# An attention and gated-MLP kernel: g factored as columns, root chains and v's split on GpSimd, the last block stored by halves

## The chip, the cores and the metric

The kernel runs on one core of one Trainium2 chip. The metric is the device time of the program in microseconds. TensorE, VectorE, ScalarE and GpSimd work side by side, each in its own order; SP issues most transfers.

## The reference

Eight batches with twelve heads of 448 positions and 64 columns go through attention with normalised queries and keys; the heads are joined to 768 columns and go through a gated channel MLP with a shift by one position. All data are float32 in the reference except what the inputs bring as 64-bit numbers: the three weight matrices.

```python
def rmsnorm(x, g):
    rms = np.sqrt(np.mean(x * x, axis=-1, keepdims=True) + 1e-06)
    return x / rms * g
q_n, k_n = (rmsnorm(q, g_q), rmsnorm(k, g_k))
scores = scale * np.matmul(q_n, k_n.transpose(0, 1, 3, 2))
attn = softmax(scores)
x = np.matmul(attn, v)                  # then joined to [8, 448, 768]
x_prev = shift(x)                       # one position later, zero first
xk = mu_k * x + (1.0 - mu_k) * x_prev
xr = mu_r * x + (1.0 - mu_r) * x_prev
k = np.maximum(xk @ w_k, 0.0)           # w_k 768 x 1024
v = k * k @ w_v                         # w_v 1024 x 768
r = 1.0 / (1.0 + np.exp(-(xr @ w_r)))   # w_r 768 x 768
return r * v
```

## The kernel before, in words

**Units and pairs.** Four heads of a batch are a unit (24 units, `u`), two heads a pair (48). A unit's k and q come as [128, 896] tiles: two heads in each half of the partitions, seven times 64 positions. `load` issues these transfers in order on SP (half of unit 0 on ScalarE's queue), `vload` those of v.

**Roots.** `stats` squares k and q (ScalarE), folds 64 columns to 32 (GpSimd), sums them (VectorE, `sst`), adds epsilon and takes the inverse root by eight small VectorE steps (`rsqrt`, line 464), whose first and fifth results lie in PSUM (`root`, a corner of the bank `last`). Unit 0 takes one chain for k and one for q; every later unit one for both, 28 columns wide. From unit 3 on (`U32`) the epsilon carries a factor from g.

**Preparing k and q.** `preps` multiplies by the roots. The first six units (`PE_T`) are then turned by TensorE (`turn`), later ones by transposing transfers. [...] The factor g_q g_k / 8 goes on k: in `turn` as one number per partition, `gc` (column 0 for the first three units, column 1, scaled by a power of g's size, for the next three), from unit 6 on as the row `G`. `setup` makes both: one product spreads g_q and g_k over the partitions, VectorE multiplies them, picks the diagonal and reduces it to `gc`, then computes the scale `gm` by a chain of one-column steps.

**Attention.** `scores` issues the products of a group (seven groups per unit) into PSUM banks `sc`; `expo` takes the row maximum (VectorE) and the exponential with its sum (ScalarE); `probs` and `split` scale and split the probabilities and turn them by transfers, or `probs_pe` by TensorE (the first 21 groups, with reciprocals in `rc`); `attends` multiplies by v in bank `last`; `settle` evacuates to `x`, for the first three units with a product that spreads the reciprocals.

**v.** `vprep` finds a power of two for v (square sum on ScalarE or maximum on VectorE, a product with an identity, a reduction, two or three steps on the bits) and from unit 3 on splits v: high part on ScalarE (line 876), low part on VectorE (line 877).

**Weights.** `wload`, `weights` and `wsplit` load 20 column slices (8 of w_k, 6 of w_r, 6 of w_v), turn their 64-bit numbers to float32, find a power of two per slice (a Gram product, its diagonal by a product with `ident`, a float32 product with ones over 128 columns, a reduction, two steps on the bits) and split them to float16, by GpSimd and ScalarE or by ScalarE and VectorE, whichever clock is behind (`LEAN_W`).

**MLP.** `mixk` and `mixr` mix x with its shift (`mix`); `moe` waits until all six pairs of a batch are mixed and all of w_k is split, multiplies by w_k, squares (`square`), and then goes over blocks of 128 rows: for each half `h` of the 768 columns the product with w_r, `gate` (tanh on ScalarE in three pieces), the product with w_v, `store`.

**What sets the order.** All of this is written as Python generators. A planner (`Plan`, line 240) keeps an estimated clock for each engine and picks at each step the operation that can start first, shifted by priorities: the constants at the head of the file, and `FIRST` and `SECOND`, which hold before batch 0's and batch 1's MLP. The instructions are then issued in that order on each engine, so an instruction that waits holds those behind it on its engine. `plan.over(a, b, d)` and `plan.lean(d)` choose an engine by these clocks. The end of a block is

```python
yield V.scalar_tensor_tensor(out=th, in0=th, scalar=1.0, in1=zv[:, 0:NH], op0=ALU.add, op1=ALU.mult)
yield G_.tensor_tensor(out=th, in0=th, in1=spread(rsu[...], P), op=ALU.mult)
if len(OC) == 2:
    for e, (r, tt) in enumerate(dst):
        yield SP.dma_start(out=r[tt], in_=o[e * HD:(e + 1) * HD, :])
```

(shortened: both halves of a block leave together, as two transfers of 64 rows).

Of the kernel before, what the change touches and what calls it, by code (L numbers as in the profile page):

```python
# [69 lines left out]
XK_AT = 2  # L70
SC_AHEAD = 0
PRIO_Q = -119
PRIO_V = 295
MARGIN = 560
MARGIN_A = 196
MARGIN_V = 569
# [8 lines left out]
BOOST_K = 564
BOOST_R = 792
BOOST_A = -32
BOOST_W = 398
# [3 lines left out]
BOOST_V = -31  # L92
SLACK_V = 2
PRIO_W = 195
W_START = 6979.55
W_G0 = -9
W_G1 = 0
PRIO_L = 233
# [14 lines left out]
LEAD_V = 0  # L113
# [80 lines left out]
def price(op):  # L194
# [5 lines left out]
    if e == "DVE":  # L200
        two = "in1" in kw
        c = n / 0.96 + (128 if two and n >= 64 and (not ps or any(SIZE[x.dtype] == 2 for x in aa)) else 64)
        return c, c + 80
# [9 lines left out]
    if "in1" in kw:  # L213
        c = n * (2.15 if kw["out"].dtype == F16 else 2.0) + 40
    else:
        c = n * 0.83 + 223
# [246 lines left out]

def rsqrt(V, y, a, t, w=None):
# [8 lines left out]
    yield V.scalar_tensor_tensor(out=y, in0=t, scalar=9.0 / 16, in1=w[1], op0=ALU.add, op1=ALU.mult)  # L473


def attn_moe_kernel(tc, q, k, v, g_q, g_k, mu_k, mu_r, w_k, w_v, w_r, out):
# [26 lines left out]
    gd = gk  # L503
# [93 lines left out]
    def setup():  # L597
# [25 lines left out]
        yield V.tensor_scalar(out=gm[:, 0:1], in0=gm[:, 0:1], scalar1=TINY, scalar2=None, op0=ALU.max)  # L623
        yield from rsqrt(V, gm[:, 1:2], gm[:, 0:1], gm[:, 5:6])
        yield V.tensor_scalar(out=G, in0=G, scalar1=gm[:, 1:2], scalar2=None, op0=ALU.mult)
        yield V.tensor_tensor(out=gc[:, 1:2], in0=gc[:, 0:1], in1=gm[:, 1:2], op=ALU.mult)
        yield V.tensor_tensor(out=gm[:, 2:3], in0=gm[:, 1:2], in1=gm[:, 1:2], op=ALU.mult)
        yield V.tensor_scalar(out=gm[:, 6:7], in0=gm[:, 1:2], scalar1=HD ** -0.5, scalar2=None, op0=ALU.mult)
        st["gm"] = True
        yield V.tensor_scalar(out=eps[:, 2 * NT:], in0=eps[:, 2 * NT:], scalar1=gm[:, 2:3], scalar2=None, op0=ALU.mult)  # L630

    def mu_stats():
# [48 lines left out]
    def stats():  # L681
        for u in range(NQ):
# [3 lines left out]
            for n, t in enumerate(LD[u]):  # L686
# [18 lines left out]
                if u == 0 or n:  # L705
# [7 lines left out]
                    if u:  # L713
                        SS[u, 0] = y
# [667 lines left out]
```

## Time and profile before

| | |
|---|---|
| median of three runs | 980.72 us (980.3 to 982.4) |
| profiled execution | 979.14 us |
| its span, first to last instruction | 977.4 us |
| TensorE matmul busy | 915.2 us (94%) |
| VectorE busy | 772.8 us (79%) |
| ScalarE busy | 756.3 us (77%) |
| GpSimd busy | 589.9 us (60%) |
| mean granted TensorE clock | 0.982 |

Busy time of TensorE is the time in which at least one matmul is under way; a matmul's own duration overlaps with that of the next. Shares over the whole span mix stages: a head in which heads are prepared and weights are split, a long middle with MLP and attention side by side, and an end with MLP products alone. [...] "Idle before" is the time an engine stood before an instruction, with what released it.

### The profile page before, as it was taken

To read this page: it belongs to the slowest core of one execution; us is meant where nothing else is said; L and a number is where in the kernel's file an instruction comes from. 1 tells how busy PE (TensorE), PEld (TensorE's weight loads), DVE (VectorE), ACT (ScalarE), POOL (GpSimd) and SP (SyncE) were. 2 spreads that over 40 slices of the span, in tenths; PEclk is the share of its full clock that TensorE was granted. 3 is DMA by queue.
4 is the path that set the end of the run, shared out by engine and by line. 5 is a ranking of instruction groups with operands and counts; after the bars stand their busy time and mean duration, and the time that the engine had idled before them with its cause. 6 is when DMAs were issued, how large, how long until landed. Compare 5 with 4: busy or idle time off the path is not lost. (4 is left out here: it accounts for less than half of the span.)

```text
span 977.4 us, 18849 instructions
## 1 busy us (share of the span) xinstructions
PE 915.2 (94%) x6171; PEld 489.2 (50%) x6171; DVE 772.8 (79%) x2132; ACT 756.3 (77%) x1818; POOL 589.9 (60%) x593
## 2 busy tenths in 40 slices
PE   3898969899999999999999999999999999999997
PEld 2554534445545554455445554455445554555564
DVE  6899899988999999888877899897989888814100
ACT  3788799989988888898987889898899888812111
POOL 2575678746767666677675558756776456425411
PEclk9799979999999999999999999999999999999999
DMA  7654389579969999899598998999799897610011
GB/s 194 165 159 134 122 211 197 125 132 200 190 132 193 208 192 188 144 182 209 108 194 167 177 175 156 171 199 173 144 178 200 162 186 145 115 24 25 1 34 32
DMA packets 399238, 147.72 MB, mean 151 GB/s; under 512 B 349476, under 2 KB 395556, under 8 KB 399140
## 3 DMA queue, kind: packets, MB, share of 16 engines
q1 hardware_dynamic: 398852, 146.06, 75.4%
q8 instruction: 48, 0.79, 0.3%
q10 hardware_dynamic: 288, 0.46, 0.2%
q14 instruction: 50, 0.41, 0.2%
HBM read 51.52 MB, written 11.01 MB: 64 GB/s over the span
## 5 line engine op out<-in xcount | busy, mean ns | idle before, releaser
L314 PE MATMUL mm<-wvh,kk 128*128 128x384 f16 x896 | 231.8, 326 | 0.0
L314 ACT ACTIVATE sc<-sc,sums 128x448 f32<-128x448 f32 x294 | 178.7, 617 | 41.5 <-DVE sums L314 36.9
L314 PE MATMUL mm<-xk,wkh 128*128 128x448 f16 x768 | 208.9, 354 | 0.8 <-DVE kf L314 0.8
L314 DVE SCALAR_TENSOR_TENSOR nat<-sc,sums,nat 128x384 f16<-128x384 f32 (+1 forms) x448 | 185.3, 462 | 24.0 <-ACT nat L314 22.7
L314 DVE TENSOR_REDUCE sums<-sc 128x1 f32<-128x448 f32 x336 | 190.2, 612 | 5.2 <-PE sc L314 4.8
L314 PEld LDWEIGHTS <-kk 128*128 128x128 f16 (+1 forms) x1362 | 130.0, 98 | 96.1 <-issue 13.8
L314 PE MATMUL mm<-wrh,xr 128*128 128x384 f16 x672 | 176.1, 328 | 0.0
L314 ACT ACTIVATE nat<-sc,sums 128x448 f16<-128x448 f32 (+1 forms) x276 | 165.5, 657 | 4.9 <-DVE sums L314 3.2
L314 PE MATMUL mm<-wvl,kk 128*128 128x384 f16 x448 | 146.0, 326 | 0.0
L314 PE MATMUL sc<-stk 64*128 64x448 f16 (+3 forms) x1104 | 128.2, 381 | 13.3 <-DVE nat L314 3.7
L314 PE MATMUL mm<-xk,wkl 128*128 128x448 f16 x384 | 135.6, 353 | 0.0
L314 PEld LDWEIGHTS <-xr 128*128 128x128 f16 x1008 | 97.4, 98 | 69.8 <-issue 7.8
L314 PE MATMUL mm<-wrl,xr 128*128 128x384 f16 x336 | 110.1, 328 | 0.0
L314 PEld LDWEIGHTS <-wkh 128*128 128x128 f16 x768 | 72.3, 98 | 75.4 <-issue 13.6
L314 PE MATMUL last<-pT,vhl 128*64 128x448 f16 x936 | 97.1, 355 | 4.9 <-DMA pT<-nat 3.5
L314 POOL TENSOR_TENSOR o<-o,bsc 128x384 f32<-128x384 f32 x48 | 40.8, 850 | 96.4 <-DVE o L314 68.7
L314 DVE SCALAR_TENSOR_TENSOR o<-o,mm 128x384 f32<-128x384 f32 x56 | 30.6, 546 | 80.8 <-PE mm L314 73.5
L314 ACT ACTIVATE o<-mm,bsc 128x128 f32<-128x128 f32 x144 | 43.3, 386 | 60.8 <-PE mm L314 36.6
L314 POOL TENSOR_TENSOR qk<-qk,ss 128x896 f32<-128x896 f32 x36 | 61.3, 1702 | 31.5 <-DVE ss L314 25.3
L314 PEld LDWEIGHTS <-vhl 128*64 128x64 f16 x936 | 51.8, 110 | 47.6 <-issue 12.0
L314 PEld LDWEIGHTS <-stk 64*128 64x128 f16 x1008 | 35.4, 98 | 69.8 <-issue 28.0
L314 POOL TENSOR_TENSOR nat<-nat 128x448 f32<-128x448 f32 x43 | 50.8, 1182 | 31.9 <-ACT nat L314 31.7
(199 smaller groups left out, 1611.0 us busy)
## 6 DMA issues: line engine op xcount, KB each, us to landing
out_dram<-o SPq DMA_DIRECT2D x56, 192.0 KB, 3.0
qk<-in_k_dram SPq DMA_DIRECT2D x46, 224.0 KB, 3.8
qk<-in_q_dram SPq DMA_DIRECT2D x36, 192.0 KB, 3.8
raw<-in_moe_w_v_dram SPq DMA_DIRECT2D x12, 512.0 KB, 4.4
raw<-in_moe_w_r_dram SPq DMA_DIRECT2D x12, 384.0 KB, 3.7
vf<-in_v_dram SPq DMA_DIRECT2D x18, 256.0 KB, 4.0
vf<-in_v_dram SPq DMA_DIRECT2D x18, 192.0 KB, 3.8
kk<-in_moe_w_k_dram SPq DMA_DIRECT2D x8, 384.0 KB, 4.0
```

The source lines that it names most:

```text
L314: r = op.fn(op.kw["out"], op.kw["value"]) if op.fn.__name__ == "memset" else op.fn(**op.kw)
```

## The change

- **g as columns.** Four one-column products put g_q and g_k on the partitions; two ScalarE steps multiply them to `gc`, which is ready before the rows. The row `G`, the scale `gm` and its root chain go to GpSimd (`rsqrt_pool`, eleven steps on tiles in SBUF).
- **Roots.** Unit 0 takes one chain for k and q together. From unit 1 on the chain goes to GpSimd when its estimated clock is behind VectorE's (`LEAN_R`), the addition of epsilon always.
- **v.** The power of two comes from one step on the exponent byte (`halfroot`), read from PSUM where v is kept whole. From unit 3 on the split goes to GpSimd (scale, subtract) with a ScalarE copy between, when GpSimd's clock is behind (`LEAN_L`).
- **Weights.** `halfroot` takes the place of two steps; for w_r and w_v the slice's scale comes from the trace of the Gram product, in one accumulating VectorE step and a one-column product.
- **Small steps moved.** mu's steps go to GpSimd or fall away, some scales and the reciprocals' offsets in `probs_pe` go to ScalarE, one inverse to GpSimd.
- **Last block.** GpSimd adds one to the gate and applies the outer scale before the w_v product is done; VectorE multiplies; each half leaves by its own two transfers.
- **Order.** Two costs of the planner are new or changed, v's loads start one unit later (`LEAD_V`), and most priorities and leanings have other values.

```diff
-LEAN_X = 0
+LEAN_X = -11
 LEAN_K = 0
+LEAN_R = 1
+LEAN_L = -7
 LEAN_W = 0
-LEAN_Q = 3000
-LEAN_M = -3000
-LEAN_V = -3000
-LEAN_H = -3000
-LEAN_N = -3736
+LEAN_Q = 2021
+LEAN_M = -1449
+LEAN_V = -2198
+LEAN_H = -2668
+LEAN_N = -5364
...
-LEAD_V = 0
+LEAD_V = 1
...
+def halfroot(V, o, a):
+    top = a.bitcast(mybir.dt.uint8).rearrange("p (n b) -> p n b", b=4)[:, :, 3]
+    return V.tensor_scalar(out=o.bitcast(I32), in0=top, scalar1=-float(1 << 23), scalar2=float(204 << 23), op0=ALU.mult, op1=ALU.add)
...
+def rsqrt_pool(G, y, a, t, u):
+    yield G.tensor_scalar(out=y.bitcast(I32), in0=a.bitcast(I32), scalar1=-0.5, scalar2=float(0x5F3759DF), op0=ALU.mult, op1=ALU.add)
+    yield G.tensor_tensor(out=t, in0=a, in1=y, op=ALU.mult)
...
+        yield [T.matmul(form=("f", 240), out=pt[h * HD:(h + 1) * HD, 2 * HD + n:2 * HD + n + 1], lhsT=g1[:, n, :], rhs=ones[0:1, :], start=True, stop=True) for n in range(2) for h in range(2)]
         yield T.matmul(form=("f", 300), out=pt[:, 0:2 * HD], lhsT=one_row, rhs=g1.rearrange("p a d -> p (a d)"), start=True, stop=True)
-        yield A.copy(out=gq, in_=pt[:, 0:HD])
+        yield A.activation(out=gc[:, 1:2], in_=pt[:, 2 * HD:2 * HD + 1], func=AF.Copy, scale=HD ** -0.5)
+        yield A.activation(out=gc[:, 0:1], in_=pt[:, 2 * HD + 1:2 * HD + 2], func=AF.Copy, scale=gc[:, 1:2])
+        st["gc"] = True
+        yield A.activation(out=gq, in_=pt[:, 0:HD], func=AF.Copy, scale=HD ** -0.5)
         yield A.copy(out=gk, in_=pt[:, HD:2 * HD])
         banks["mm"].put(pt)
-        yield V.scalar_tensor_tensor(out=G, in0=gq, scalar=1.0 / float(HD) ** 0.5, in1=gk, op0=ALU.mult, op1=ALU.mult)
-        for h in range(2):
-            hs = slice(h * HD, (h + 1) * HD)
-            yield V.tensor_tensor(out=gd[hs, :], in0=G[hs, :], in1=ident[hs, hs], op=ALU.mult)
-        yield V.tensor_reduce(out=gc[:, 0:1], in_=gd, axis=AX.X, op=ALU.add)
-        st["gc"] = True
+        yield G_.tensor_tensor(out=G, in0=gq, in1=gk, op=ALU.mult)
...
+        yield from rsqrt_pool(G_, gm[:, 1:2], gm[:, 0:1], gm[:, 5:6], gm[:, 4:5])
+        yield G_.tensor_scalar(out=G, in0=G, scalar1=gm[:, 1:2], scalar2=0.0, op0=ALU.mult, op1=ALU.add)
...
-                if u == 0 or n:
-                    c = slice(2 * NT * n if u == 0 else 0, 2 * NT * (n + 1))
-                    if u < U32:
-                        yield V.tensor_scalar(out=ss[:, c], in0=ss[:, c], scalar1=1e-6, scalar2=None, op0=ALU.add)
+                if n:
+                    c = slice(0, NSS)
+                    E_ = G_ if u and plan.over("POOL", "DVE", LEAN_R) else V
+                    if not u:
+                        yield V.tensor_scalar(out=ss, in0=ss, scalar1=1e-6, scalar2=None, op0=ALU.add)
+                    elif u < U32:
+                        yield G_.tensor_scalar(out=ss[:, c], in0=ss[:, c], scalar1=1.0, scalar2=1e-6, op0=ALU.mult, op1=ALU.add)
                     else:
-                        yield V.tensor_tensor(out=ss, in0=ss, in1=eps, op=ALU.add)
-                    yield from rsqrt(V, y[:, c], ss[:, c], tm[:, c], (root[:, 0, c], root[:, 1, c]))
-                    SS[u, n] = y
-                    if u:
-                        SS[u, 0] = y
+                        yield G_.tensor_tensor(out=ss, in0=ss, in1=eps, op=ALU.add)
+                    if E_ is G_:
+                        yield from rsqrt_pool(G_, y[:, c], ss[:, c], tm[:, c], su[:, c])
+                    else:
+                        yield from rsqrt(V, y[:, c], ss[:, c], tm[:, c], (root[:, 0, c], root[:, 1, c]))
+                    SS[u, 0] = SS[u, 1] = y
...
+        m = vs[:, 2:3] if half else pt[:, 2 * P:2 * P + 2]
+        yield V.tensor_reduce(out=m, in_=pt[:, 0:n * P].rearrange("p (a c) -> p a c", c=P), axis=AX.X, op=ALU.max)
+        if half:
+            banks["ot"].put(pt)
...
+            yield halfroot(V, sv, m)
...
-                yield A.activation(out=hl[:, 0], in_=ve, func=AF.Copy, scale=sv)
-                yield V.scalar_tensor_tensor(out=hl[:, 1], in0=ve, scalar=sv, in1=hl[:, 0], op0=ALU.mult, op1=ALU.subtract)
+                if plan.over("POOL", "DVE", LEAN_L):
+                    yield G_.tensor_scalar(out=ve, in0=ve, scalar1=sv, scalar2=0.0, op0=ALU.mult, op1=ALU.add)
+                    yield A.copy(out=hl[:, 0], in_=ve)
+                    yield G_.tensor_tensor(out=hl[:, 1], in0=ve, in1=hl[:, 0], op=ALU.subtract)
+                else:
+                    yield A.activation(out=hl[:, 0], in_=ve, func=AF.Copy, scale=sv)
+                    yield V.scalar_tensor_tensor(out=hl[:, 1], in0=ve, scalar=sv, in1=hl[:, 0], op0=ALU.mult, op1=ALU.subtract)
...
-            yield V.tensor_scalar(out=r, in0=sums[:, 4:7:2] if u >= U32 else r, scalar1=1e-9, scalar2=2.0 ** -15, op0=ALU.add, op1=ALU.mult)
+            yield A.activation(out=r, in_=sums[:, 4:7:2] if u >= U32 else r, func=AF.Copy, scale=2.0 ** -15, bias=1e-9 * 2.0 ** -15)
...
+        if ci < NF:
+            yield V.tensor_tensor(out=dg, in0=pg[:, 0:P], in1=ident, op=ALU.mult)
+            yield T.matmul(form=("f", 400), out=pg[:, P:2 * P], lhsT=ones.broadcast_to([P, P]), rhs=dg, start=True, stop=True)
+            R["dg"].put(dg)
+            yield V.tensor_reduce(out=sc, in_=pg[:, P:2 * P], axis=AX.X, op=ALU.max)
+            banks[WB(ci)].put(pg)
+            yield halfroot(V, sc, sc)
+        else:
+            tr = small.tile([P, 1], F32, name="trace", bufs=2)
+            yield V.tensor_tensor_reduce(out=dg, in0=pg[:, 0:P], in1=ident, scale=1.0, scalar=0.0, op0=ALU.mult, op1=ALU.add, accum_out=tr)
+            R["dg"].put(dg)
+            yield T.matmul(form=("f", 250), out=pg[:, P:P + 1], lhsT=ones.broadcast_to([P, P]), rhs=tr, start=True, stop=True)
+            yield halfroot(V, sc, pg[:, P:P + 1])
+            banks[WB(ci)].put(pg)
...
-            yield V.tensor_scalar(out=RSC, in0=WIN[:, 0:NF], scalar1=wsc[:, 0:1], scalar2=RELU_SCALE, op0=ALU.mult, op1=ALU.mult)
+            yield V.tensor_scalar(out=wsc[:, 0:1], in0=wsc[:, 0:1], scalar1=RELU_SCALE, scalar2=None, op0=ALU.mult)
+            yield A.activation(out=RSC, in_=WIN[:, 0:NF], func=AF.Copy, scale=wsc[:, 0:1])
...
+                    last = b == B - 1 and blk == NT - 1
+                    plan.spawn(gate(h, zr, th, rsu, TH, last), PRIO_M)
...
+        if last:
+            yield G_.tensor_scalar(out=th, in0=th, scalar1=1.0, scalar2=1.0, op0=ALU.mult, op1=ALU.add)
+            yield outer(h, th, rsu)
         TH[0] = True
 
-    def store(h, zv, th, rsu, o, OC, dst, TH):
+    def outer(h, th, rsu):
+        t3 = th.rearrange("p (c n) -> p c n", n=P)
+        return G_.tensor_tensor(out=t3, in0=t3, in1=spread(rsu[:, ND + 3 * h:ND + 3 * h + 3], P), op=ALU.mult)
...
+        if last:
+            yield V.tensor_tensor(out=th, in0=th, in1=zv[:, 0:NH], op=ALU.mult)
+            banks["mm"].put(zv)
+            for e, (r, tt) in enumerate(dst):
+                yield SP.dma_start(out=r[tt][:, h * NH:(h + 1) * NH], in_=th[e * HD:(e + 1) * HD, :])
+            return
```

## Rows read from the trace of the kernel before

**Rows 1.** Windows: stretch, length, each engine's busy time (instructions), clock, DMA share, GB/s.

```profile
20.00:200.00 180.00, 152.01 (x1002) 83.97 (x1000) 163.40 (x436) 151.94 (x340) 121.49 (x121) 0.91 0.62 158
200.00:850.00 650.00, 636.51 (x4424) 330.87 (x4419) 572.88 (x1614) 572.54 (x1398) 421.62 (x408) 1.00 0.93 172
...
122.40:145.50 23.10, 14.24 (x99) 7.72 (x98) 20.67 (x59) 20.89 (x42) 17.50 (x17) 0.74 0.82 210
```

**Rows 2.** Timeline, 119 to 146 us: start, duration, engine, operation, tiles; [idle before <- releaser].

```profile
119.23 3.23 PE L314 MATMUL last<-pT,vf 128*64 128x448 f32 x16
...
141.22 0.68 DVE L314 TENSOR_SCALAR sc<-x,bsc 128x448 f32<-128x448 f32 x1
...
145.46 0.93 PE L314 MATMUL mm<-xk,wkh 128*128 128x448 f16 x2
```

**Rows 3.** Timeline of the first 20 us.

```profile
7.77 0.76 PE L314 MATMUL mm<-grow,ones 1*128 1x128 f32 x2 [7.77 <-DMA grow<-in_g_k_dram]
8.26 1.12 POOL L314 TENSOR_TENSOR nat<-nat 128x448 f32<-128x448 f32 x1 [0.67 <-ACT nat L314]
8.28 1.14 DVE L314 TENSOR_SCALAR sst<-sst 128x14 f32<-128x14 f32 x1
...
10.90 0.17 DVE L314 SCALAR_TENSOR_TENSOR ss<-stm,last 128x14 f32<-128x14 f32 x1
10.98 0.61 DVE L314 TENSOR_REDUCE sst<-nat 128x14 f32<-128x448 f32 x1
11.51 1.08 DVE L314 TENSOR_TENSOR nat<-xk,ss 128x896 f32<-128x896 f32 x1
...
12.74 1.73 PE L314 MATMUL sc<-ident,nat 128*128 128x128 f32 x7 [4.21 <-DVE sst L314]
...
15.69 0.69 ACT L314 ACTIVATE stk<-sc,gc 128x512 f32<-128x512 f32 x1 [6.79 <-DVE gc L314]
...
19.27 2.45 PE L314 MATMUL sc<-stk 64*128 64x448 f32 x8
```

**Rows 4.** Groups of VectorE instructions by shape, 0 to 200 us: busy us, mean ns | idle.

```profile
L314 DVE TENSOR_SCALAR WSC<-WSC 128x1 int32<-128x1 int32 x40 | 5.8, 144 | 0.2
...
L314 DVE SCALAR_TENSOR_TENSOR vhl<-vf,bstat,vhl 128x512 f16<-128x512 f32 x4 | 3.4, 838 | 0.5 <-ACT vhl L314 0.5
L314 DVE TENSOR_TENSOR dg<-mm,ident 128x128 f32<-128x128 f32 x12 | 3.3, 279 | 0.1
...
L314 DVE TENSOR_TENSOR sst<-sst,eps 128x28 f32<-128x28 f32 x4 | 2.6, 658 | 0.1
L314 DVE TENSOR_TENSOR stm<-sst,last 128x28 f32<-128x28 f32 x10 | 1.8, 180 | 0.2
...
L314 DVE TENSOR_SCALAR rc<-rc 128x8 f32<-128x8 f32 x3 | 1.4, 456 | 0.0
```

**Rows 5.** Groups of GpSimd and ScalarE instructions by shape, whole span.

```profile
L314 POOL TENSOR_TENSOR nat<-qk,nat 128x512 f16<-128x512 f32 x10 | 11.6, 1158 | 4.7 <-ACT nat L314 4.7
...
L314 POOL TENSOR_SCALAR raw<-raw 128x512 int32<-128x512 uint8 x12 | 8.3, 691 | 1.8 <-DMA raw<-in_moe_w_v_dram 1.0
...
L314 POOL COPY x<-x 128x63 f32<-128x63 f32 x24 | 5.7, 237 | 33.5 <-DVE x L314 25.6 <-ACT x L314 5.2 <-DVE sums L314 2.6
L314 POOL TENSOR_TENSOR nat<-qk,nat 128x128 f16<-128x128 f32 x13 | 5.6, 427 | 0.0
...
L314 ACT ACTIVATE bsc<-ismu,bsc 128x2 f32<-128x2 f32 x8 | 2.6, 321 | 1.1 <-DVE bsc L314 1.1
```

**Rows 6.** Timeline of the end, from 967 us.

```profile
967.66 0.89 ACT L314 ACTIVATE o<-mm,bsc 128x128 f32<-128x128 f32 x3 [5.89 <-PE mm L314]
...
971.63 0.55 DVE L314 SCALAR_TENSOR_TENSOR o<-o,mm 128x384 f32<-128x384 f32 x1 [6.19 <-PE mm L314]
972.27 0.83 POOL L314 TENSOR_TENSOR o<-o,bsc 128x384 f32<-128x384 f32 x1 [5.91 <-DVE o L314]
973.12 1.11 SPq L314 DMA_DIRECT2D out_dram<-o  x2
```

More of the change, by code (lines that the diff above doesn't have):

```diff
@@ L69 @@
 MU_AT = 1
-XK_AT = 2
+XK_AT = 3
 SC_AHEAD = 0
-PRIO_Q = -119
-PRIO_V = 295
+PRIO_Q = -127
+PRIO_V = 299
 MARGIN = 560
-MARGIN_A = 196
-MARGIN_V = 569
+MARGIN_A = 293
+MARGIN_V = 612
 PS = 0.1
@@ L80 @@
 PRIO_K = -112
-PRIO_R = 342
-PRIO_O = 57
+PRIO_R = 324
+PRIO_O = 220
 O_BUFS = 2
 PRIO_M = 490
[L85 to L88, printed above, removed]
+BOOST_K = 486
+BOOST_R = 262
+BOOST_A = -66
+BOOST_W = 222
 BOOST_Q = 898
@@ L91 @@
 SLACK_Q = 3
[L92 to L95, printed above, removed]
+BOOST_V = -66
+SLACK_V = 1
+PRIO_W = 228
+W_START = 6604.274
 W_G0 = -9
 W_G1 = 0
-PRIO_L = 233
+PRIO_L = 106
 Q_DVE = 1
@@ L201, in price @@
         two = "in1" in kw
-        c = n / 0.96 + (128 if two and n >= 64 and (not ps or any(SIZE[x.dtype] == 2 for x in aa)) else 64)
+        if kw.get("accum_out") is not None:
+            return n / 0.96 + 190, n / 0.96 + 270
+        ap = any(isinstance(kw.get(k), bass.AP) for k in ("scalar", "scalar1")) and n > 2 and SIZE[kw["out"].dtype] == 4
+        c = n / 0.96 + 60 * ap + (128 if two and n >= 64 and (not ps or any(SIZE[x.dtype] == 2 for x in aa)) else 64)
         return c, c + 80
@@ L213, in price @@
     if "in1" in kw:
-        c = n * (2.15 if kw["out"].dtype == F16 else 2.0) + 40
+        c = n * (2.15 if kw["out"].dtype == F16 else 2.0) + (40 if n > 300 else 150)
     else:
@@ L502, in attn_moe_kernel @@
     gc = const.tile([P, 2], F32, name="gc")
-    gd = gk
     NW = NF + 2 * ND
@@ L629, in setup @@
+        yield G_.tensor_tensor(out=gm[:, 2:3], in0=gm[:, 1:2], in1=gm[:, 1:2], op=ALU.mult)
+        yield G_.tensor_scalar(out=gm[:, 6:7], in0=gm[:, 1:2], scalar1=HD ** -0.5, scalar2=0.0, op0=ALU.mult, op1=ALU.add)
         st["gm"] = True
-        yield V.tensor_scalar(out=eps[:, 2 * NT:], in0=eps[:, 2 * NT:], scalar1=gm[:, 2:3], scalar2=None, op0=ALU.mult)
+        yield G_.tensor_scalar(out=eps[:, 2 * NT:], in0=eps[:, 2 * NT:], scalar1=gm[:, 2:3], scalar2=0.0, op0=ALU.mult, op1=ALU.add)
     def mu_stats():
@@ L692, in stats @@
                 yield A.activation(out=xs, in_=tv, func=AF.Square, scale=gm[:, 6:7] if n and u >= U32 else HD ** -0.5)
-                yield G_.tensor_tensor(out=xs[:, :, 0:HD // 2], in0=xs[:, :, 0:HD // 2], in1=xs[:, :, HD // 2:], op=ALU.add)
-                m = HD // 2
+                m = HD
+                if True:
+                    m //= 2
+                    yield G_.tensor_tensor(out=xs[:, :, 0:m], in0=xs[:, :, 0:m], in1=xs[:, :, m:2 * m], op=ALU.add)
                 while m > 1 and (u, n) in TREE and m > TREE_TO:
@@ L1189, in weights, with inverse @@
             plan.spawn(wsplit(nm, kt, c, ci, f), wprio)
-    def inverse(o, i):
-        return V.tensor_scalar(out=o.bitcast(I32), in0=i.bitcast(I32), scalar1=-1.0, scalar2=float(0x7F000000), op0=ALU.mult, op1=ALU.add)
+    def inverse(o, i, E=V):
+        return E.tensor_scalar(out=o.bitcast(I32), in0=i.bitcast(I32), scalar1=-1.0, scalar2=float(0x7F000000), op0=ALU.mult, op1=ALU.add)
     def wsplit(nm, kt, c, ci, f):
@@ L1201, in wsplit @@
         sc = WSC[:, ci:ci + 1]
-        sci = sc.bitcast(I32)
         dg = yield from R["dg"].get()
-        yield V.tensor_tensor(out=dg, in0=pg[:, 0:P], in1=ident, op=ALU.mult)
-        yield T.matmul(form=("f", 400), out=pg[:, P:2 * P], lhsT=ones.broadcast_to([P, P]), rhs=dg, start=True, stop=True)
-        R["dg"].put(dg)
-        yield V.tensor_reduce(out=sc, in_=pg[:, P:2 * P], axis=AX.X, op=ALU.max)
-        banks[WB(ci)].put(pg)
-        yield V.tensor_scalar(out=sci, in0=sci, scalar1=24, scalar2=23, op0=ALU.logical_shift_right, op1=ALU.logical_shift_left)
-        yield V.tensor_scalar(out=sci, in0=sci, scalar1=-1.0, scalar2=float(204 << 23), op0=ALU.mult, op1=ALU.add)
+        if ci < NF:
[5 more added lines that the diff above has]
+            yield halfroot(V, sc, sc)
+        else:
+            tr = small.tile([P, 1], F32, name="trace", bufs=2)
[4 more added lines that the diff above has]
+            banks[WB(ci)].put(pg)
         if plan.over("POOL", "DVE", LEAN_W):
@@ L1331, in square, with gate @@
         KF[f] = True
-    def gate(h, zr, th, rsu, TH):
+    def gate(h, zr, th, rsu, TH, last):
         for c in range(3):
```

54 lines of the change are left out of this document (28 added, 26 removed).

## The prediction

> **What bounds the kernel now.** I read the windows of the trace first, then the timeline where TensorE stands. From 200 us on TensorE has work nearly all the time: between 200 and 850 us it is busy 636.5 of 650 us at a granted clock of 1.00 [rows 1]. The change leaves its large products as they are, so this part can give back at most 13.5 us. Time is left in three places: the start, the head up to about 200 us, and the tail behind the last product.
>
> In the head, 20 to 200 us, TensorE is idle 180 - 152.0 = 28.0 us, and its mean clock is 0.91 [rows 1]. [...] The fullest engine there is VectorE, 163.4 of 180 us (0.908), then ScalarE with 151.9 and GpSimd with 121.5. The worst piece is 122.4 to 145.5 us: TensorE 14.2 of 23.1 us at clock 0.74, VectorE and ScalarE 20.7 and 20.9 [rows 1]. There the MLP's first product waits for batch 0's last head pair: that pair's value product starts at 119.23 and lasts 3.23, its mix comes to VectorE only at 141.22, and the MLP starts at 145.46 [rows 2]. The steps between are a few us of work; the rest is queueing on VectorE and ScalarE behind weight splits and other heads. So I take the head as bound by VectorE's load.
>
> **The start.** Today k's evacuation waits 6.79 us for `gc`, which comes through VectorE at about 15.6, and the first scores start at 19.27 [rows 3]. With the change `gc` is two one-column ScalarE steps behind the g product. That starts at 7.77 [rows 3]; allowing 0.8 for it and 2 x 0.32 for the steps (the 128x2 row of [rows 5]), `gc` is there by 9.3. The four added one-column products stand in the 4.21 us that TensorE idles before 12.74 [rows 3] and cost nothing; without that cover they cost under 1 us. The price is that k now waits for q: one chain for both. GpSimd's fold of q ends at 8.26 + 1.12 = 9.38, the reduction (0.61) at about 10.0. Eight chain steps took from 8.28 + 1.14 = 9.42 to 11.07 today, so with an addition of 0.2 they end at 11.9. The two multiplications of 1.08 end at 13.0 and 14.1, q's seven transposes (1.73) at 15.9, the last evacuation (0.69) at 16.6 [rows 3]. First scores at 16.6 instead of 19.27: -2.7 us, with 0 and -3.3 as ends. Loading v one unit later moves unit 1's k and q ahead of two pairs of v transfers in SP's queue, and v behind them; v's own squares can slip, since the value products come after all of a pair's scores. I put 0 on it.
>
> **The head's load.** Off VectorE, in 20 to 200 us [rows 4]: five root chains of eight steps at 0.18 = 7.2, with four eps additions at 0.658 = 2.6; one power-of-two step less in each of 20 weight slices, 20 x 0.145 = 2.9; in 12 slices a product with the identity (0.28) and a reduction that I take as long become one accumulating step. No row shows that form: between 0.28 and 0.56, I take 0.42, the middle, so 12 x 0.14 = 1.7. v's low parts are four at 0.838 = 3.4 at most, the reciprocals' offsets 6 x 0.456 = 2.7, v's roots three steps, 0.5, and the remainder of g's and mu's chains some 17 steps at 0.18 = 3. Sum 24.0 of 163.4, leaving 139; the bounds are 12 (half of the choices by clock stay on VectorE) and 27.
>
> On ScalarE: about 11 small steps at 0.32 [rows 5] = +3.5, making 155.5. On GpSimd: five chains of 11 steps, five eps steps and some 16 of the setup, 76 small ones. The nearest rows are a 128x63 copy at 0.237 and a 128x128 two-input step at 0.427 [rows 5]; 28 elements are nearer the first, so 0.25: 19 us, with 32 as the upper end and, at VectorE's 0.18, 14 as the lower. v's splits add up to 4 x (0.69 + 1.16) = 7.4 [rows 5]. GpSimd comes to 121.5 + 26 = 148 of 180, with 161 at the upper end.
>
> So ScalarE becomes the fullest, 155.5 us. If the head shrinks until ScalarE stands at VectorE's 0.908 of today, it lasts 155.5 / 0.908 = 171 us: -9 us. Ends: 0, if the order of issue and not the load sets it, and -22, half of the 44 us that TensorE loses there. The change also sets new priorities and leanings for that order; no row of before shows what they do. I price them inside these ends, and on the other side by half a stall like that of [rows 2], some +10.
>
> **GpSimd's new queue.** The chain's steps stand in GpSimd's order behind its longer pieces, and its own scaling of k and q waits for them. In the steady part this happens units ahead of use. The trace also shows VectorE and GpSimd holding each other up: the addition on `sst` took 1.14 us beside GpSimd's fold [rows 3], and the four eps additions 0.658 in the mean, while chain steps with an operand in PSUM stay at 0.18 [rows 4]. [...]
>
> **Middle and tail.** In the middle VectorE loses some 2 us in each later unit. Of 13.5 us idle I take 1.5 back (ends +4 and -6).
> Behind the last product, which ends near 971.5, stand VectorE 0.55, GpSimd 0.83 and two stores, with 0.09 between the first two [rows 6]. For the last block GpSimd's two steps (I take the 128x512 one-input 0.69 for the first, 0.83 the second) go ahead, beside the value product: ScalarE's gate starts at 967.66 and takes 0.89 [rows 6], so 971.5 - 968.6 = 2.9 us of cover stand against 1.5 of work. Without it, up to 0.9 comes back. The gain is 0.83 + 0.09 = 0.9; the stores, half as large, may give 0 to 0.4, I take 0.1: -1.0.
>
> **The sum.** Against the profiled execution, 979.14 us: -2.7 - 9 - 1.5 - 1.0 = -14.2, which is 964.9. The median of the runs, 980.72, lies 1.6 above that execution, so 966.5.
>
> **The rivals.**
> 1. Only start and tail: the order of issue sets the head. For it: the last pair waited although each engine still had gaps of 10% [rows 1, 2]. Against: those gaps are small, and 24 us of work goes. 979.14 - 2.7 - 1.0 + 1.6 = 977.0.
> 2. Slower: GpSimd becomes the head's bound. With small steps at 0.427 and 0.25 of waiting each (half the 0.48 by which the eps additions exceed 0.18), 76 x 0.68 = 51 us and 7.4 for v make 180 us of work; at 0.908 full the head lasts 198: +18 - 2.7 - 1.0 + 1.6, which is 995. It turns slower from about 42 us of added GpSimd work. Against: 26 is likelier, and what is chosen by clock goes to VectorE when GpSimd is behind.
> 3. Nothing to measure: the start's gain is waited away at transfers, or the new order loses in the middle what the head gains: about 980.
> 4. More: the shorter queue also keeps TensorE's clock up and half of the head's 44 us comes back: -22 - 2.7 - 1.0 - 1.5 + 1.6, which is 953.5.
>
> **How the numbers follow.** Forecast 0.57, rival 1 0.13, rival 4 0.12: faster 0.82. Rival 3 0.08: the same. Rival 2 0.10: slower. About 0.2% (2 us) is what can be told from no change. The range from 953 to 980 leaves out rival 2 and part of rival 4.
>
> **What would show it.** Right: `gc` before 10 us; first scores near 16.6; the first MLP product by about 133 to 138; TensorE's idle time in the head under 22 us; from the last product to the end 4.9 instead of 5.9 us. Wrong: GpSimd's small steps over 0.4 us, GpSimd over 90% full before the MLP starts, the first MLP product at 145 us or later, or more than 20 us idle on TensorE between 200 and 850 us.

## The result and the profile after

The changed kernel takes 966.01 us in the median of four runs (964.35 to 967.81), the kernel before in the same rounds 981.11: a ratio of 0.9845, interval 0.9824 to 0.9866. The profiled execution of the changed kernel took 965.76 us with a span of 964.0, against 979.14 and 977.4: 13.4 us less. The forecast was 966.5. The total came out; the terms did not, as the next views show.

Windows of the changed kernel, the stretches of [rows 1] (length; busy us of TensorE, its weight loads, VectorE, ScalarE, GpSimd; clock, DMA share, GB/s):

```profile
20.00:200.00 180.00, 151.18 (x1018) 81.47 (x1018) 153.81 (x350) 148.19 (x343) 125.08 (x173) 0.93 0.64 154
200.00:850.00 650.00, 643.10 (x4478) 336.90 (x4476) 539.67 (x1445) 571.64 (x1404) 496.94 (x625) 1.00 0.92 173
```

In the head TensorE stands idle for 28.8 us, before for 28.0 [rows 1]: no gain in idle time, only in clock, 0.93 for 0.91. Most of that lies between 20 and 40 us (windows before, then of the changed kernel):

```profile
20.00:40.00 20.00, 15.06 (x81) 9.44 (x78) 18.67 (x59) 12.89 (x33) 7.84 (x8) 0.77 0.54 149
```
```profile
20.00:40.00 20.00, 15.82 (x98) 8.47 (x98) 17.95 (x37) 18.23 (x48) 11.60 (x20) 1.00 0.70 176
```

Before, TensorE was busy for only 0.62 of the 2 us from 30 to 32, the clock fell there, to 0.73 in the mean, and it stood at 0.50 from 32 to 40 us; this one fall costs 3.5 us of work by 40 us (15.1 us busy, 11.6 us of work at full clock). In the changed kernel it did not come (clock 1.00 from 20 to 40 us), though TensorE was busy for only 0.52 of the 2 us from 34 to 36. In the middle TensorE's idle time has halved, from 13.5 [rows 1] to 6.9 us.

Idle time alone hides the clock, so I also counted how far TensorE has come: its busy time times the granted clock, added up over windows of 10 us, in us of work at full clock.

| done by | 20 us | 60 | 80 | 150 | 200 | 400 | 850 |
|---|---|---|---|---|---|---|---|
| before | 5.1 | 34.3 | 53.1 | 99.8 | 143.8 | 339.9 | 780.3 |
| after | 5.9 | 40.6 | 56.9 | 108.0 | 148.3 | 346.1 | 791.4 |
| lead | 0.8 | 6.3 | 3.8 | 8.2 | 4.5 | 6.2 | 11.1 |

The lead is 4.5 us at 200 us and 11.1 at 850. The end behind the last product gives 1.5 (below), and the remaining 0.8 of the 13.4 is what is left over: summed to the last product, TensorE's work is 901.6 us before and 901.0 after, which fits the twelve products over 128 columns that became products over one (busy 6.5 us before and 4.6 after, with 0.6 for the four new products of g). So: start and head together 4.5, middle 6.6, end 1.5.

These are sizes of one execution of each kernel. Two later runs keep the changed kernel's order through the whole middle (`t_old` and `s_hold` below); their profiled executions did 639.1 and 641.1 us of work between 200 and 850 us, against 643.1 here and 636.5 before. By these three the middle's gain is 2.6 to 6.6 us, and the other terms carry scatter too.

Timeline of the changed kernel to the first scores, to be held against [rows 3] (start, duration, engine, operation; [idle before <- releaser]):

```profile
8.48 0.17 ACT L319 ACTIVATE gc<-mm 128x1 f32<-128x1 f32 x1
...
8.69 0.26 ACT L319 ACTIVATE gc<-mm,gc 128x1 f32<-128x1 f32 x1
...
12.39 0.18 DVE L319 SCALAR_TENSOR_TENSOR ss<-stm,last 128x28 f32<-128x28 f32 x1
12.60 1.09 DVE L319 TENSOR_TENSOR nat<-xk,ss 128x896 f32<-128x896 f32 x1
13.84 1.73 PE L319 MATMUL sc<-ident,nat 128*128 128x128 f32 x7 [5.39 <-DVE gm L319]
...
15.68 0.62 DVE L319 TENSOR_SCALAR stk<-sc,gc 128x384 f32<-128x384 f32 x1 [1.67 <-PE sc L319]
16.21 1.08 DVE L319 TENSOR_TENSOR nat<-xk,ss 128x896 f32<-128x896 f32 x1
17.35 1.76 PE L319 MATMUL sc<-ident,nat 128*128 128x128 f32 x7 [1.57 <-DVE nat L319]
19.55 3.08 PE L319 MATMUL sc<-stk 64*128 64x448 f32 x8
```

`gc` is there at 8.95, yet the first scores start at 19.55, not earlier than 19.27 [rows 3]. VectorE multiplies k (12.60), then stands 1.67 us for k's transposes, evacuates k (15.68) and only then multiplies q (16.21), whose roots were ready at 12.57. Before, VectorE evacuated k at the same time:

```profile
15.70 0.62 DVE L314 TENSOR_SCALAR stk<-sc,gc 128x384 f32<-128x384 f32 x1
```

There k's transposes ended at 12.74 + 1.73 = 14.47 [rows 3], so `gc` held VectorE's evacuation up by 1.2 us at most. Now k waits for q's sums, its transposes start 1.1 us later (13.84 for 12.74), and the two cancel.

The MLP of batch 0 starts at 130.0 instead of 145.46 [rows 2]:

```profile
130.03 0.93 PE L319 MATMUL mm<-xk,wkh 128*128 128x448 f16 x2
```

Timeline of the end, against [rows 6]:

```profile
956.76 0.51 POOL L319 TENSOR_SCALAR o<-o 128x384 f32<-128x384 f32 x1 [5.29 <-ACT o L319]
957.36 0.83 POOL L319 TENSOR_TENSOR o<-o,bsc 128x384 f32<-128x384 f32 x1
...
959.32 0.33 PE L319 MATMUL mm<-wvh,kk 128*128 128x384 f16 x1
959.79 0.55 DVE L319 TENSOR_TENSOR o<-o,mm 128x384 f32<-128x384 f32 x1 [6.21 <-PE mm L319]
960.37 1.11 SPq L319 DMA_DIRECT2D out_dram<-o  x2
```

GpSimd's two steps now end at 958.19, over a microsecond ahead of the last product's end at 959.65, and the stores follow VectorE's step directly. From that end to the end of the span it is 964.0 - 959.65 = 4.3 us.

GpSimd's new small steps, groups by shape over the whole span (busy us, mean ns | idle before):

```profile
L319 POOL TENSOR_SCALAR stm<-stm 128x28 f32<-128x28 f32 x38 | 9.6, 253 | 3.3
...
L319 POOL TENSOR_SCALAR ss<-sst 128x28 int32<-128x28 int32 x19 | 4.1, 213 | 1.7
```

The chains' steps take 0.21 to 0.25 us in the mean. 19 of the 23 chains of the later units went to GpSimd (the x19 of the chain's first step).

### The profile page after: what moved, and what is told of

It is laid out like the page before. It is cut to its first block, busy times and chain, and to the rows that moved or that the text cites. A ratio compares the mean times of both kernels' runs of the same rounds, so it can differ in the third digit from the quotient of the medians.

```text
span 964.0 us, 18880 instructions
## 1 busy us (share of the span) xinstructions
PE 909.8 (94%) x6179; PEld 486.2 (50%) x6179; DVE 723.9 (75%) x1856; ACT 753.9 (78%) x1828; POOL 672.4 (70%) x882
## 5 line engine op out<-in xcount | busy, mean ns | idle before, releaser
L319 DVE SCALAR_TENSOR_TENSOR nat<-sc,sums,nat 128x384 f16<-128x384 f32 (+2 forms) x444 | 183.2, 463 | 42.2 <-ACT nat L319 41.5
L319 PE MATMUL mm<-xk,wkh 128*128 128x448 f16 x768 | 211.3, 357 | 3.4 <-DVE kf L319 2.4
L319 PEld LDWEIGHTS <-kk 128*128 128x128 f16 (+1 forms) x1362 | 129.8, 98 | 95.8 <-issue 13.4
L319 POOL TENSOR_TENSOR nat<-qk,nat 128x768 f16<-128x768 f32 (+3 forms) x58 | 59.0, 1035 | 13.9 <-ACT nat L319 13.6
L319 POOL TENSOR_TENSOR nat<-nat 128x448 f32<-128x448 f32 x40 | 46.8, 1171 | 29.5 <-ACT nat L319 23.0
```

Of the source, the lines that this page charges most:

```text
L319: r = op.fn(op.kw["out"], op.kw["value"]) if op.fn.__name__ == "memset" else op.fn(**op.kw)
```

## The experiments

Two theories stood after this. **Theory A**, that of the forecast: the head is bound by VectorE's load, so load put back on VectorE costs its time, and the same load on a less full engine, GpSimd above all, costs little. **Theory B**: the order of issue binds it; every engine's queue is on some path, so a delay on any of them passes on, and what the change won lies as much in its new order as in the moved work. For the middle, A said that VectorE's load counts for a part only.

To load an engine without changing the order, I let small steps without a reader ("ballast") follow given instructions on that engine; all other instructions keep the changed kernel's order on every engine. The planner doesn't know of them. What a run costs is its ratio less 0.9845, times 981 us (where an expectation names the cost of an earlier run, it is the plain difference of the medians, up to 3 us less); the intervals of both ratios leave 2.5 to 4 us on each such number.

### Ballast on VectorE in the head

```diff
+def LOAD(u, i):
+    return 2 if 0 < u < 6 and i < 9 else 0
...
+    ballast = lambda: nc.vector.tensor_reduce(out=idle[:, 0:1], in_=idle[:, 1:NSS], axis=AX.X, op=ALU.max)
...
-                        yield from rsqrt_pool(G_, y[:, c], ss[:, c], tm[:, c], su[:, c])
+                        for i, op in enumerate(rsqrt_pool(G_, y[:, c], ss[:, c], tm[:, c], su[:, c])):
+                            op.extra = [ballast] * LOAD(u, i)
+                            yield op
```

(`op.extra` is issued right behind the operation, here on VectorE behind its last instruction. The chains themselves run on GpSimd, so this ballast lies beside them and not in them.)

> The changed kernel with two short VectorE reductions (28 columns, no reader, about 0.15 us each) put behind each of the first nine steps of the five GpSimd root chains of units 1 to 5: 90 steps, some 13.5 us of VectorE time, all before 200 us. Every engine's order of all other instructions is that of the changed kernel. If the head is bound by VectorE's load, as the prediction had it, the time rises by 5 to 10 us and the first MLP product comes that much later. If the order of issue and the length of chains set the head, 0 to 2 us.

The group of the ballast:

```profile
L711 DVE TENSOR_REDUCE idle<-idle 128x1 f32<-128x27 f32 x90 | 16.0, 178 | 2.0
```

Measured 978.51 us, ratio 0.9990 [0.9975, 1.0005]: 14.2 us for 16.0 us, 0.89 per us, and nearly all that the change had won. The work done by 80 us is 50.1 instead of 56.9. By itself this speaks for A.

### The same load elsewhere in the head: other VectorE work, ScalarE, GpSimd

Behind `halfroot` in `wsplit`, away from the root chains:

```diff
-            yield halfroot(V, sc, sc)
+            hr = halfroot(V, sc, sc)
+            hr.extra = [ballast] * 5
+            yield hr
```

(and the same for the slices with a trace.)

> The changed kernel with five of the short VectorE reductions behind each of the 20 weight slices' power-of-two steps: 100 steps, some 18 us, between 35 and 175 us, off the root chains; the order of all else is kept. Ballast in the root chains cost 12.5 us on VectorE and 14.7 on GpSimd, which GpSimd's 125 of 180 busy us don't explain. If VectorE's load is what counts, this costs 8 us or more. If it was the delay of the root chains of units 1 and 2, which the trace shows as 7 us lost by 80 us, this costs under 4.

On ScalarE and GpSimd, at the same places as the first (i < 8). On GpSimd the ballast lies in the chains: each next step of a chain waits behind it.

```diff
+    ballast = lambda: nc.scalar.copy(out=idle, in_=idle)
...
+    ballast = lambda: nc.gpsimd.tensor_scalar(out=idle, in0=idle, scalar1=1.0, scalar2=0.0, op0=ALU.mult, op1=ALU.add)
```

> The changed kernel with two short ScalarE copies (128 x 28, some 0.2 us each) issued behind each of the first eight steps of the root chains of units 1 to 5: 80 steps, some 17 us, before 200 us, in no chain; order of all else kept. If only the root chains' delay counts, under 4 us. If every engine's order is so tight in the head that any delay is passed on, 8 us or more, as on VectorE and GpSimd. If VectorE alone is the bound, under 4 us too; then the case with weights tells.

> The changed kernel with two short GpSimd steps (128 x 28, no reader, about 0.21 us each) behind each of the first eight steps of the five GpSimd root chains of units 1 to 5: 80 steps, some 17 us, before 200 us; the order of all else is unchanged. If GpSimd has room in the head, as the prediction had it (125 of 180 us busy), the time rises by 0 to 3 us, against 12.5 for 16 us on VectorE. If GpSimd had become the bound, or its steps hold VectorE up, 8 us or more.

Groups of the ballast, in this order:

```profile
L711 DVE TENSOR_REDUCE idle<-idle 128x1 f32<-128x27 f32 x100 | 17.9, 179 | 2.8
```
```profile
L711 ACT COPY idle<-idle 128x28 f32<-128x28 f32 x80 | 17.1, 213 | 1.8
```
```profile
L711 POOL TENSOR_SCALAR idle<-idle 128x28 f32<-128x28 f32 x80 | 19.3, 242 | 4.0
```

| ballast in the head | us added | ratio | cost, us | per us | work by 200 us |
|---|---|---|---|---|---|
| VectorE, beside the chains | 16.0 | 0.9990 [0.9975, 1.0005] | 14.2 | 0.89 | 139.4 |
| VectorE, at the weights | 17.9 | 0.9983 [0.9970, 0.9996] | 13.5 | 0.76 | 139.1 |
| ScalarE, beside the chains | 17.1 | 0.9977 [0.9962, 0.9992] | 12.9 | 0.76 | 138.0 |
| GpSimd, in the chains | 19.3 | 1.0021 [1.0001, 1.0041] | 17.3 | 0.90 | 135.3 |

Three engines with different loads (VectorE 153.8, ScalarE 148.2, GpSimd 125.1 of 180 us after the change) give the same price within what can be told. Against the changed kernel, TensorE has lost up to 200 us, in the order of the table, 5.8, 8.7, 5.3 and 8.0 us to idle time and 3.0, 0.4, 5.0 and 4.9 us to a lower clock, so the price holds both.

That VectorE alone is the bound falls for the changed kernel: with the order held, ScalarE's time costs as much, though its ballast lies in no chain. That GpSimd's time is as dear, on an engine with a fifth less to do than VectorE, fits B, but there the delay of the chains and the load can't be told apart: TensorE waits 6.1 us at `sc` for GpSimd's `nat`, which the roots are multiplied into, and ballast on GpSimd away from the chains was not run. The price doesn't come through VectorE being slowed: the VectorE instructions that the changed kernel starts by 200 us take 186.6 us in sum there, and the same ones 185.4 with ballast on GpSimd. The ballast was not tried in the kernel before, so whether VectorE's share mattered more there stays open.

### Ballast in the middle

The same with `u > 5`: on VectorE (i < 9), and on GpSimd (i < 7).

> The same ballast in the middle: two reductions behind each of nine steps of the 14 GpSimd root chains of units 6 and later, 252 steps, some 38 us, which brings VectorE from 540 us between 200 and 850 us to about 578, near the 573 of before. Order of all else as in the changed kernel. If VectorE's relief is what took TensorE's idle time there from 13.5 to 6.9 us, the time rises by 4 to 8 us. If transfers and the new order did it, 0 to 2 us. As the prediction sized it: 1.5 us.

> The changed kernel with two short GpSimd steps behind each of the first seven steps of the 14 GpSimd root chains of units 6 and later: 196 steps, some 47 us, between 200 and 850 us; the order of all else is kept. 45 us on VectorE there cost 23.5 us. GpSimd is busy 497 of these 650 us. If VectorE's load is what bounds the middle behind TensorE, this costs under 6 us. If any delay on any engine is passed on, 15 us or more.

VectorE: 44.9 us added, ratio 1.0091 [1.0060, 1.0122], 24.1 us, 0.54 per us. GpSimd: 42.9 us added, ratio 1.0167 [1.0145, 1.0189], 31.6 us, 0.74 per us. On VectorE that is three times the upper end of what was expected; on GpSimd it is the second case, any delay is passed on. TensorE's idle time in the stretch is 23.9 us with ballast on VectorE and 29.5 on GpSimd, where it was 6.9, and the clock, 0.99 in the mean, takes another 5.8 and 6.9 us. So I read who released TensorE between 200 and 850 us. The waits of TensorE in that stretch (engine, tile, what released it: total us, times, longest), first before:

```profile
PE sc L314 <- DVE nat L314: 3.7, 6, 1.1
PE last L314 <- DMA pT<-nat: 3.5, 5, 1.0
PE sc L314 <- DVE df L314: 2.4, 2, 1.4
PE sc L314 <- DVE dfx L314: 0.6, 1, 0.6
...
```

then the changed kernel:

```profile
PE last L319 <- DMA pT<-nat: 2.7, 5, 0.9
...
PE sc L319 <- DVE natx L319: 0.5, 1, 0.5
...
PE sc L319 <- DVE nat L319: 0.4, 2, 0.2
...
```

then that with ballast on GpSimd:

```profile
PE sc L319 <- DVE nat L319: 13.2, 11, 2.5
...
PE sc L319 <- DVE natx L319: 3.3, 4, 1.2
...
```

TensorE waited 6.7 us for VectorE at `sc` (`nat`, `df` and `dfx`); with the change 0.9 is left (`nat` and `natx`), a fall nearly of the size of the middle's gain, 6.6. In the executions of `t_old` and `s_hold` 3.2 and 1.9 us are left. Ballast on VectorE brings such waits back (11.0 us for `nat`, 3.2 for `natx`, 1.8 for `df`); so does ballast on GpSimd, though VectorE itself has no more to do there. A score bank is freed by VectorE, but what stands ahead of that in VectorE's order also waits for GpSimd. The trace bears this out in part: with ballast on GpSimd, VectorE waits 7.4 us for GpSimd at `df` where it waited 1.1, and ScalarE 24.3 us for GpSimd's `qk` at `nat` and `natx` where it waited 1.4; that these waits reach the score banks is my reading.

### Code and constants apart

The changed code with the constants of before (`LEAN_R` and `LEAN_L` as in the change), and the code of before with the new constants.

```diff
-LEAN_X = -11
+LEAN_X = 0
...
-LEAD_V = 1
+LEAD_V = 0
```

> The code of the changed kernel with every priority, leaning and start time of before (LEAN_R and LEAN_L, which before does not have, stay at 1 and -7). The work that is moved off VectorE is the same; the order is the one that the old constants give. If the moved work is the gain, 966 to 973 us, at least half of the 15 us. If the new constants are the gain, 976 us or more.

> The code of before with the constants of the changed kernel: no work moved, only the order and the leanings. If the moved work is the gain, 976 us or more, since VectorE keeps its load and the new leanings put more on it. If the constants are the gain, 972 us or less.

New code with old constants: 972.23 us, ratio 0.9916 [0.9884, 0.9948], 8.2 us faster than before. Old code with new constants: 1005.85 us, 1.0261 [1.0236, 1.0285], 25.6 us slower. Windows of the latter:

```profile
20.00:200.00 180.00, 144.25 (x950) 77.77 (x948) 162.09 (x419) 140.87 (x315) 104.14 (x111) 0.91 0.57 146
200.00:850.00 650.00, 625.15 (x4308) 325.09 (x4304) 567.75 (x1581) 554.88 (x1350) 437.45 (x432) 0.98 0.91 172
```

Its TensorE has done 757.0 us of work by 850 us, 23 less than before. The constants win nothing alone; on the new code they are worth the 7 us between 8.2 and 15.2. About half of the gain is the moved work as the old priorities order it. The waits of the middle go the same way: TensorE's for VectorE's `nat`, `natx`, `df` and `dfx` at `sc` are 3.3 us with the new code and the old constants, 6.9 before, and 12.1 with the old code and the new constants.

### The planner's order alone

One number that only the plan sees, a latency in its estimated clocks, one unit up:

```diff
-    LAT = 35
+    LAT = 36
```

> The changed kernel with nothing changed but the planner's assumed latency between engines, 36 instead of 35 ns: the same instructions, some of them in another order. It shows how far the time moves by re-planning alone. If the 15 us come from the work that was moved, it stays within 3 us of the changed kernel. If they come from an order that happens to fit, it gives back 5 us or more.

968.85 us, ratio 0.9875 [0.9848, 0.9902]: 2.9 us slower than the changed kernel, with the same work in another order and a few steps chosen for another engine (VectorE's instructions are 1871 for 1856). The intervals just overlap, so read it as a size: another order of equal standing moves the time by some 3 us.

### q's multiplication ahead of k's turn

First in the generator, both multiplications ahead of both turns for unit 0 (`Q_DVE` is 1), with a new plan:

```diff
+            if u < Q_DVE:
+                both = []
+                for n, t in enumerate(LD[u]):
...
+                    both.append((w, nat))
+                for n, (w, nat) in enumerate(both):
+                    yield from turn(w, X, n, u)
```

> The changed kernel with unit 0's second multiplication by the roots (q) issued right behind the first (k), ahead of k's turn and evacuation. The predicted 2.7 us at the start did not come: first scores at 19.55 us against 19.27. The theory is that q's multiplication stands behind k's evacuation in VectorE's order, where the engine idles 1.67 us: here the first scores should start at about 17.4 us and the time fall by 1 to 2 us, to about 964.5, with some 3 us of scatter from the new order. The rival is that something else holds the scores (q's own path): first scores still at 19 us or later.

```profile
16.67 2.53 PE L319 MATMUL sc<-stk 64*128 64x448 f32 x8
```

The first scores start at 16.67, as the forecast had said of the change (16.6), and TensorE is 3.1 us ahead of the changed kernel at 60 us. Yet the run takes 991.21 us, 1.0112 [1.0080, 1.0143]. The new plan loses it later:

```profile
200.00:250.00 50.00, 38.84 (x264) 19.28 (x265) 40.28 (x111) 41.55 (x101) 25.57 (x24) 0.83 0.96 179
```

(the window from 200 to 250 us), by a lower clock, 0.83 where the changed kernel has 1.00, and by TensorE's waits, between 200 and 300 us above all:

```profile
PE sc L319 <- DVE nat L319: 8.7, 4, 5.2
```

So the swap was made again with the order held: only k's evacuation on VectorE and q's multiplication change places, in unit 0.

```diff
-                    yield V.tensor_scalar(out=dst, in0=src, scalar1=gc[:, 0:1], scalar2=None, op0=ALU.mult)
+                    ev = V.tensor_scalar(out=dst, in0=src, scalar1=gc[:, 0:1], scalar2=None, op0=ALU.mult)
+                    ev.hold = u == 0
+                    yield ev
...
+                    ml.free = u == 0 and n == 1
```

(a held step is issued behind the next free one.)

> The changed kernel with unit 0's q multiplication moved ahead of the one VectorE piece of k's evacuation, and not one other instruction moved on any engine: the start of the version that came out at 991 us, without its new order. There the first scores started at 16.67 us, where the prediction had put them, and 17 us were lost between 200 and 300 us. If the start is worth what the prediction took it for, the first scores come at about 17.5 us and the time falls by 1 to 2.5 us. If the head swallows it, 0.

```profile
17.66 1.77 PE L322 MATMUL sc<-stk 64*128 64x448 f32 x8
```

The first scores start 1.9 us earlier. In the median of five runs it takes 962.5 us, ratio 0.9817 [0.9793, 0.9841], the lowest of all versions, but its runs spread from 962.33 to 967.22, its interval meets that of the changed kernel, and in its profiled execution (967.22) nothing of the lead is left at 200 us (148.1 us of work against 148.3). The three runs near 962.4 had a mean granted clock of 0.989 or 0.990, the two slower ones 0.985 and 0.986, the changed kernel 0.988. Whether the earlier start reaches the end stays open.

### The old end

```diff
-                    last = b == B - 1 and blk == NT - 1
+                    last = False
```

> The changed kernel with the last block handled as every other block: outer scale on GpSimd behind VectorE's product, both halves leaving together. The order before the last block is the same. The trace of the changed kernel has 4.35 us behind the last product against 5.87 before, so the theory expects +1.5 us (the prediction said 1.0); if the tail was shortened by something else, 0.

```profile
963.65 0.33 PE L319 MATMUL mm<-wvh,kk 128*128 128x384 f16 x1
...
964.72 0.83 POOL L319 TENSOR_TENSOR o<-o,bsc 128x384 f32<-128x384 f32 x1 [5.91 <-DVE o L319]
965.57 1.11 SPq L319 DMA_DIRECT2D out_dram<-o  x2
```

Its span ends at 969.8: 5.8 us behind the last product's end at 963.98, against 4.3 with the change. From the first store to the end it is 4.2 us, with the half stores 3.6. The whole run takes 968.57 us (0.9879 [0.9844, 0.9914]), 3.3 us more, but the profiled execution lost some 3.5 us of TensorE's work by 850 us, in instructions of the same order (787.9 against 791.4): that is scatter from run to run, and only the 1.5 us behind the last product are the edit's.

## Why the prediction was right, point by point

The time was right; the sum that led to it was right in sign and wrong in most of its terms, which made up for one another. That the total came out within a microsecond is luck.

| term | forecast | measured |
|---|---|---|
| start | -2.7 | 0 (first scores at 19.55 for 19.27) |
| head to 200 us | -9 | -4.5, all of it clock |
| middle | -1.5 | -6.6 (-2.6 and -4.6 in `t_old` and `s_hold`) |
| end | -1.0 | -1.5 |
| less work on TensorE | not counted | some -0.8 |

- **The start.** `gc` came at 8.95 (by 9.3 forecast), the chain ended at 12.57 (11.9). The step that failed is "the two multiplications of 1.08 end at 13.0 and 14.1": it counted when the operands are there, not what stands ahead on VectorE. `preps` turns k before it multiplies q, so q's multiplication stood behind k's evacuation, as it had before. The 6.79 us by which the forecast had k's evacuation wait for `gc` were ScalarE's idle time; only some 1.2 of them lie behind the end of k's transposes. With the two changed over the first scores came at 16.67 and 17.66. The bound of 0 held.
- **The head's load.** VectorE lost 163.4 - 153.8 = 9.6 us between 20 and 200 us instead of 24, less than the lower bound of 12. The step that failed took the choices by clock as they had been: when VectorE's clock falls back, the planner gives it work. The low parts of the weight slices show it:

```profile
L319 DVE SCALAR_TENSOR_TENSOR wkl<-wf,WSC,wkh 128x768 f16<-128x768 f32 x4 | 5.4, 1344 | 0.1
L319 DVE SCALAR_TENSOR_TENSOR wvl<-wf,WSC,wvh 128x1024 f16<-128x1024 f32 x3 | 4.2, 1398 | 0.4 <-ACT wvh L319 0.4
L319 DVE SCALAR_TENSOR_TENSOR wrl<-wf,WSC,wrh 128x768 f16<-128x768 f32 x3 | 3.9, 1285 | 0.2 <-ACT wrh L319 0.2
...
L319 DVE CUSTOM_DVE_ANT_0 dg<-mm,ident 128x128 f32<-128x128 f32 x12 | 3.4, 280 | 0.0
L319 DVE SCALAR_TENSOR_TENSOR wkl<-kk,WSC,wkh 128x768 f16<-128x768 f32 x3 | 3.3, 1099 | 0.0
...
L319 DVE DVE_READ_ACCUMULATOR2_ANT trace<- 128x1 f32 x12 | 1.0, 83 | 0.0
```

  (groups of VectorE in the changed kernel, 20 to 200 us.) 13 low parts, 16.8 us, lie on VectorE, where before there were 7 with 7.9. GpSimd was freed of 16.2 us in turn (weight low parts and the scalings ahead of them, 36.1 to 19.9 us): it grew by 3.6 us (121.5 to 125.1), not by 26, and it made one of v's low parts in the head, not four.
- **"So I take the head as bound by VectorE's load."** This is the reason that fell. A fuller queue was read as the bound, but ballast costs 0.76 to 0.90 per us on each of three engines (GpSimd's with the chains' delay in it). The scaling "until ScalarE stands at 0.908" had no ground, and the idle time, which it should have cut to 22 us, stayed at 28.8. What came was the clock, which rival 4 names: 0.93 for 0.91 of 180 us is 3.6 us. About as much came from the one fall between 30 and 40 us that did not come; no run tells what kept it away, and two runs whose work by 60 us is nearly the changed kernel's (`n_lat` and `s_hold`) stood at 0.86 and 0.83 in those 10 us. The MLP started at 130.0, earlier than the 133 to 138 forecast, but 3.7 us of the lead of 8.2 at 150 us were lost again by 200. Of the 44 us that the forecast halves for its low end, 28.0 are idle time; the other 16 are an estimate, 0.09 of 180 us, which no run shows: by the windows of 10 us the lower clock took 13.4 us in the head before, and 8.8 after.
- **The middle.** Here the mechanism was right as far as the waits show (VectorE loses work in every unit) and the term mis-sized, -1.5 for -6.6 in the profiled execution and -2.6 in the least good one of the same order. It was a part of the 13.5 us of idle, taken without looking at who ended those waits. Their view was there: 6.7 us by VectorE at `sc`, which the change relieves (VectorE 572.9 to 539.7 us). With the new code and the old constants (`k_old`) TensorE's idle time there is 10.0 us, so about half of the fall from 13.5 to 6.9 came with the moved work alone, within the scatter named above.
- **The end.** The 0.83 + 0.09 for GpSimd's step came as forecast, with more cover than needed. The half stores gave 0.6 us, above the 0 to 0.4.
- **The sizes.** GpSimd's small steps, 0.25 forecast, took 0.21 to 0.25 in the mean; the accumulating step, 0.42 forecast, 0.280 and 0.083 for reading the sum out, 0.36.
- **The rivals.** Rival 2 (GpSimd becomes the bound) did not come: no chain step over 0.253 in the mean (single ones up to 1.09, below), and the planner took other work off GpSimd. That work on GpSimd can cost is real, though, as 19.3 us there cost 17.3. Rival 1's reason, the order of issue, was the better account of the head as far as these runs go; its time, 977, was not, for the middle gained. Of rival 4 the clock's part came in small.

What stays open is how the gain divides between less work and a better order. Ballast prices work that is added to a fixed order, not what its removal buys when all is planned anew; the constants gave 7 us on the new code and took 26 on the old.

## What to carry to other kernels

The fullest engine of a stretch is not thereby its bound (here VectorE, 153.8 of 180 us, where a us of ballast cost 0.76 to 0.89, and on ScalarE, with 148.2, 0.76): ask for each wait of the engine that counts who ended it, and price a piece of work by putting some of it back with the order held. In a kernel whose order a planner makes, freed time on one engine is filled by its own choices (13 low parts on VectorE in the head for 7), and a new plan moved the time by 3 to 26 us here, so judge a small edit with the order fixed. An operand that is ready earlier helps only if nothing stands ahead of its reader in the program's order: `gc` came at 8.95 instead of about 15.6 us, and the first scores at 19.55 instead of 19.27.

## What the runs showed of the hardware

GpSimd's 28-column chain steps kept means of 0.213 to 0.253 us over the whole kernel, while some of VectorE's small steps on SBUF were held up. Timeline of VectorE, then of GpSimd, at the same time in the changed kernel:

```profile
186.42 1.76 DVE L319 TENSOR_SCALAR WIN<-WIN,smu 128x6 f32<-128x6 f32 x1
188.09 1.17 DVE L319 TENSOR_SCALAR WIN<-WIN,wsc 128x6 f32<-128x6 f32 x1
...
189.77 0.21 DVE L319 TENSOR_SCALAR WIN<-WIN,wsc 128x6 f32<-128x6 f32 x1
```
```profile
186.46 1.69 POOL L319 TENSOR_TENSOR nat<-qk,ss 128x896 f32<-128x896 f32 x1
188.11 1.12 POOL L319 TENSOR_TENSOR nat<-nat 128x448 f32<-128x448 f32 x1
```

The same six columns take 1.76, 1.17 and 0.21 us. The first two end 0.03 us behind the GpSimd step beside them (186.46 + 1.69 = 188.15, 188.11 + 1.12 = 189.23), the third has none beside it. TensorE's next products at `sc` start at 188.20. The trace puts 2.5 us of that wait down to `WIN`, but the products read `nat`, which GpSimd finished at 188.15, and their weight load waited for it:

```profile
188.20 0.42 PEld L319 LDWEIGHTS sc<-ident,nat 128*128 128x128 f32 x4 [2.90 <-POOL nat L319]
```

So no time of TensorE's is shown to hang on the held steps.

It goes the other way too. GpSimd's one-input steps of 0.21 us, an addition of epsilon and two chain steps, were held up three times in the changed kernel's head (0.92, 0.86 and 1.09 us), each time beside a VectorE step with two inputs in SBUF, a weight slice's low part, that had started 0.17 to 0.50 us earlier; GpSimd's step ends 0.07 or 0.08 us behind it. VectorE, then GpSimd:

```profile
165.21 1.52 DVE L319 SCALAR_TENSOR_TENSOR wvl<-wf,WSC,wvh 128x1024 f16<-128x1024 f32 x1
```
```profile
165.71 1.09 POOL L319 TENSOR_SCALAR stm<-stm 128x28 f32<-128x28 f32 x1
```

So small GpSimd steps wait too, which no row of before shows. In these three cases VectorE's step had started first, and GpSimd's ended with it. On VectorE's side the starts in the trace don't settle who goes first: its two steps start 0.04 and 0.02 us before GpSimd's and still end with them. In all five the small step ends 0.03 to 0.08 us behind the other engine's step; what makes it wait, the runs don't show.
